# A convolution and an ELU feed-forward layer on one core: another route for the first super tile, and a new order of loads and output turns at the start

## The chip, the cores and the metric

The kernel runs on one core of one Trainium2 chip. Time is device microseconds of one execution; the number that counts is the median over runs. Engines: PE (TensorE; its weight loads are PEld), DVE (VectorE), ACT (ScalarE), POOL (GpSimd) and SP (SyncE, which here only issues DMAs).

## The reference, cut to what matters

```
x: 8 x 4096 x 192 (fp32), weight: 8 heads x 7 taps
w = softmax(weight, over the 7 taps)
a[b, s, h*24 + c] = sum over k of w[h, k] * x[b, s + k - 6, h*24 + c]   # zeros ahead of each batch row
h = a @ w_in            # 32768 x 192  @  192 x 2048
g = h if h > 0 else exp(min(h, 0)) - 1
out = g @ w_out         # 32768 x 2048 @ 2048 x 192, fp32
```

A causal convolution of seven taps along the sequence, one set of taps for each of eight heads of 24 channels; then a feed-forward layer with an ELU.

## The kernel before, in words

The 32768 tokens are 32 super tiles (`s`) of 1024 tokens, each in two groups of 512 (`GS`). The hidden 2048 columns are 16 blocks of 128 (`q`); a step `n = 16 s + q` makes one block of hidden values for both groups, and there are 512 steps. The array is used as two row halves (`tile_position` 0 and 64): the two groups of tokens lie on partitions 0 to 63 and 64 to 127, with the 192 channels cut into three pieces `j` of 64. For that w_in is held twice, in the lower and in the upper 64 rows.

**Convolution** (L622, "c" items). x is loaded by POOL with a cast to bf16 into `xg`, as overlapping windows of 118 tokens, 112 of them new. A banded matrix `Tm` (118 x 112 for each head) turns a window into 112 convolved tokens. A super tile has four convolution units `m`, two heads each, with matmuls on the rows below and above 64. Each unit is evacuated to `csb` (L522 on ACT), and one DMA transpose (L412, issued by SP) then brings the super tile into `att`, channel-major, as the H matmuls need it. The units of super tile s are run some 20 steps ahead of their use, at `CONV_AT`; those of s=1 at the steps `EARLY_CONV`; those of s=0 ahead of everything.

**The band.** The taps are softmaxed on DVE and ACT (`wq` to `wprb`). SP writes zeros to a DRAM tensor `conv_band`, then writes `wprb` along its diagonal, then reads it back into `Tk` (tap-major layout, 128 rows of 1792 bytes). Super tile 0 is convolved with `Tk`; DVE copies it into `Tm` (L561) for the rest.

**H** (L643). Three matmuls of 512 columns (j = 0, 1, 2) for each group; ACT takes exp of the PSUM bank into `E` (L526); POOL clamps E to at most 1 (L499); DVE forms `max(E - 1, H)` into `gT` as fp16 (L575). That is the ELU. A unit of this chain is one (n, group).

**Output** (L666, "o" items). For each half super tile `k` and group `g`, 64 matmuls accumulate over the 16 q in one PSUM bank, in turns of `QB` = 2 blocks a step, starting at step `O_AT` = 12 for group 0 and 16 for group 1. The bank is evacuated by ACT (L530) and stored by SP (L369).

**Order.** A planner in Python at the head of the kernel writes out PE's order: every item gets a due time from a model clock for each row half, items of a step are interleaved by it, and PSUM's eight banks are given out in the order in which the model believes them free. Each engine then works through its own list in order; semaphores hold the dependencies, and PE waits (`wait_bank`) for whatever last used a bank. `warm` puts matmuls on zeros (L605) into the order: 40 at the start, 24 ahead of the first H, two in each of the steps 1 to 11.

**Order of loads.** POOL issues x of super tile 0, the first 8 blocks of w_in (lower rows), waits for them and copies them to the upper rows by DMA, waits for DVE's second csb evacuation, issues x of super tile 1, waits for the transposed `att`, and issues the other half of w_in. x of super tile 2 and w_out are issued among the first steps (`x_before`, `W_OUT_AT`). SP copies the other half of w_in to the upper rows (L716).

Of the kernel before, what the change touches and what calls it, by code (L numbers as in the profile page):

```python
# [27 lines left out]
CU = 4  # L28
# [9 lines left out]
QA = 8  # L38
WARM = (40, 24, 2)
# [6 lines left out]
EARLY_CONV = (3, 4, 6, 7)  # L46
X_AT = ((2, 1, 1), (1, 1, 0))
ZERO_AT = 8
W_OUT_AT = 5
X_EARLY = 7  # L50
X_WHOLE = False
X_OFF = 0


def bass_lightweight_conv__then__act_elu_kernel(
# [100 lines left out]
    def warm(count):  # L156
        what = ("w", len(plan))
        take_bank(what)
        freed[bank_of[what]] = max(clock)
        plan.append((max(clock) - AHEAD, what + (count,)))  # L160
        clock[:] = [max(clock)] * 2
# [11 lines left out]
    def block_items(n, g, rt):  # L173
        k, b = divmod(n - O_AT[g], NB)
        if k < 0:
            return []
        items = o_items(k, g, rt, range(QB * b, QB * (b + 1)), 2 * b + rt, True, True)
        return evacuated(items, k, g) if b == NB - 1 and rt == 1 else items
# [7 lines left out]
    warm(WARM[0])  # L186
    for rt in range(2):
        lists = [[], []]
        for m in range(CU):
            lists[rt] += c_items(m, rt)  # L190
        emit(lists)
        clock[:] = [max(clock)] * 2
    for n in range(NP):
        if n == 0:
            warm(WARM[1])
        elif n < O_AT[0]:
            warm(WARM[2])
        lists = [[], []]
        convs = conv_steps.get(n, [])
        for m in convs:  # L200
            lists[0] += c_items(m, 0)
        lists[0] += block_items(n, 0, 0) + block_items(n, 1, 0) + h_items(n, 0)
        lists[1] += h_items(n, 1)
        for m in convs:
            lists[1] += c_items(m, 1)
        lists[1] += block_items(n, 0, 1) + block_items(n, 1, 1)
        emit(lists)
# [21 lines left out]
    emit(tail)  # L229
    pe_order += [item for _, item in sorted(plan, key=lambda p: p[0])]  # L230
# [24 lines left out]
    x_before = {4: [(2, 0)]}  # L255
    for s in range(2, NS):
        for u, ahead, gr in X_AT:
            before = 0
            for item in act_order:
                before += item[0] == "h"  # L260
                if item == ("c", CU * s + u):
                    break
            if s + ahead < NS:
                x_before.setdefault(before + X_OFF, []).append((s + ahead, gr))
    x_before.setdefault(X_EARLY, []).append((2, 1))
# [4 lines left out]
    band = nc.dram_tensor("conv_band", (P, TW, HEADS), BF16).ap()  # L270

    with ExitStack() as stack:
# [11 lines left out]
        Tk = sbuf("Tk", [P, CW, HEADS], BF16)  # L284
# [8 lines left out]
        wq = sbuf("wq", [P, HEADS, KSIZE], FP32)  # L293
        wmx = sbuf("wmx", [P, HEADS], FP32)
        wq2 = sbuf("wq2", [P, HEADS, KSIZE], FP32)
        wex = sbuf("wex", [P, HEADS, KSIZE], FP32)
        wsum = sbuf("wsum", [P, HEADS], FP32)
        wrs = sbuf("wrs", [P, HEADS], FP32)
        wprb = sbuf("wprb", [P, KSIZE, HEADS], BF16)
# [5 lines left out]
        s_w = [sema(f"s_w{i}") for i in range(3)]  # L305
# [4 lines left out]
        s_tm = sema("s_tm")  # L310
        s_cd = sema("s_cd")
        s_wdp = sema("s_wdp")
# [30 lines left out]
        WCOLS = ((0, P * QA), (P * QA, FF))  # L343
        def x_whole(s):
            return X_WHOLE and 2 < s < NS - 1

        x_need, z_need, z_count = {}, {}, 0
        x_count = [[0, 0] for _ in range(NXB)]
        for s in range(NS):
            z_count += s % SPB == 0  # L350
            z_need[s] = z_count
            for g in range(2):
                if g == 0 or not x_whole(s):
                    x_count[s % NXB][g] += 16 + 16 * ((s, g) in ((0, 0), (NS - 1, 1)))
                x_need[s, g] = x_count[s % NXB][g]

        by_vector = (1, 3)

        def conv_read(W, m):

            if m in by_vector:
                W(s_cd, by_vector.index(m) + 1)
            else:
                W(s_ce, m + 1 - sum(v < m for v in by_vector))
# [9 lines left out]
        def conv_evac(W, m):  # L374

            s, u = divmod(m, CU)
            if s >= 2:
                W(s_att[s % 2], 16 * (s // 2))
# [39 lines left out]
        def _gpsimd(g: bass.BassGpSimd):  # L418
            W = Waits(g)

            def load_x(s, gr):
                b = s % NXB
                if s >= NXB:
                    W(s_cv, CU * (s - NXB) + CU)
                if s == 0 and gr == 0:
                    g.memset(xg[0:PAD, 0, 0, :], 0.0).then_inc(s_z)
                    g.dma_start(
                        xg[PAD:KW, 0, 0, :], x_flat[0 : KW - PAD, :]
                    ).then_inc(s_x[0][0], 16)

                if x_whole(s):
                    if gr == 0:
                        src = bass.AP(
                            tensor=x_flat.tensor,
                            offset=(s * SUP - PAD) * D,
                            ap=[[D, P], [CW * D, NWIN], [GS * D, 2], [1, D]],
                        )
                        g.dma_start(
                            xg[:, b, :, :].rearrange("p (w g) d -> p w g d", g=2), src
                        ).then_inc(s_x[b][0], 16)  # L440
                    return

# [13 lines left out]
                else:  # L456
                    windows(int(s == 0 and gr == 0), NWIN, P)
# [6 lines left out]
            def load_w_in(k):  # L464
                c0, c1 = WCOLS[k]
                for j in range(3):
                    g.dma_start(  # L467
                        w_in[0:HP, j, c0:c1],
# [7 lines left out]
            for gr in range(2):  # L476
                load_x(0, gr)
            load_w_in(0)
            W(s_w[0], 48)
            c0, c1 = WCOLS[0]  # L480
            g.dma_start(w_in[HP:P, :, c0:c1], w_in[0:HP, :, c0:c1]).then_inc(s_wdp, 16)  # L481
            W(s_cd, 2)
            for gr in range(2):
                load_x(1, gr)
            W(s_att[0], 16)
            load_w_in(1)
            for i, (n, u) in enumerate(units):
                s, at_n = divmod(i // 2, NQ)
                if i % 2 == 0:
                    if i // 2 == W_OUT_AT:  # L490
                        g.dma_start(
                            w_out[:, :, :], moe_w_out.rearrange("(q p) d -> p q d", p=FC)
                        ).then_inc(s_w[2], 16)
                    if at_n == ZERO_AT and (s + 2) % SPB == 0 and s + 2 < NS:
                        batch_zeros(s + 2)
# [13 lines left out]
        def _scalar(a):  # L509
            W = Waits(a)  # L510
            a.memzero(scr[:, 0:1]).then_inc(s_scr)
# [3 lines left out]
            a.activation(wex[:], wq2[:], ACT.Exp).then_inc(s_wex)  # L515
            for item in act_order:
                if item[0] == "c":
                    m = item[1]
                    if m in by_vector:
                        continue  # L520
                    W(s_cv, m + 1)
# [13 lines left out]
        def _vector(v):  # L535
            W = Waits(v)
            v.memset(zw[:], 0.0).then_inc(s_zw)  # L537
            W(s_wq, 16)
# [5 lines left out]
                wmx[:, :].unsqueeze(2).to_broadcast([P, HEADS, KSIZE]),  # L544
# [6 lines left out]
            W(s_set, 4)  # L551
            v.tensor_tensor(  # L552
                wprb[:, ::-1, :].rearrange("p k h -> p h k"),
                wex[:],
                wrs[:, :].unsqueeze(2).to_broadcast([P, HEADS, KSIZE]),
                ALU.mult,
            ).then_inc(s_set)
            for m in by_vector:
                W(s_cv, m + 1)
                v.tensor_copy(*conv_evac(W, m)).then_inc(s_cd)  # L560
            v.tensor_copy(  # L561
                Tm[0:KW, :, :].rearrange("p h t -> p t h"), Tk[0:KW, :, :]
            ).then_inc(s_tm)
# [21 lines left out]
        def _tensor(pe):  # L585
            W = Waits(pe)

            def wait_bank(what):
# [3 lines left out]
                if was[0] == "h":  # L592
                    W(s_tt, tt_count(*was[1:]))
                elif was[0] == "c":
# [5 lines left out]
            for item in pe_order:  # L600
                if item[0] == "w":
                    W(s_zw, 1)
                    wait_bank(item[:2])
                    for _ in range(item[2]):
                        pe.matmul(H[:, bank_of[item[:2]], :], zw[:, 0:P], zw[:, 0:GS], start=True, stop=True)  # L605
                elif item[0] == "c":
                    _, m, rt, q = item
                    s, u = divmod(m, CU)
                    if m == 0:
                        W(s_band, 48)  # L610
                    if m == CU:
                        W(s_tm, 1)
# [5 lines left out]
                    else:  # L618
                        W(s_cswap, m + 1)
# [4 lines left out]
                        Tm[rows, h, :] if s else Tk[rows, :, h],  # L624
# [9 lines left out]
                elif item[0] == "h":  # L634
                    _, n, r, j = item
                    s, q = divmod(n, NQ)
                    if j == 0:
                        W(s_w[q // QA], 48)
                        if r == 1:
                            W(s_wdp if q < QA else s_wd, 16)  # L640
                        W(s_att[s % 2], 16 * (s // 2 + 1))
                        wait_bank(item[:3])
                    ins = pe.matmul(  # L643
# [9 lines left out]
                else:  # L653
# [9 lines left out]
                    W(s_w[2], 16)  # L663
# [17 lines left out]
        def _sync(sy):  # L681
            W = Waits(sy)
            sy.dma_start(
                wq[:, :, :].rearrange("p h k -> p (h k)"),
                bass.AP(tensor=weight.tensor, offset=0, ap=[[0, P], [1, HEADS * KSIZE]]),
            ).then_inc(s_wq, 16)
            W(s_zw, 1)
            sy.dma_start(
                band[:, :, :].rearrange("p t h -> p (t h)"), zw[:, :]
            ).then_inc(s_band, 16)  # L690
            W(s_band, 16)
            W(s_set, 5)
# [3 lines left out]
                ap=[[HEADS * (TW + 1), P], [1, KSIZE * HEADS]],  # L696
            )
            sy.dma_start(
                diagonal, wprb[:, :, :].rearrange("p k h -> p (k h)")
            ).then_inc(s_band, 16)  # L700
            W(s_band, 32)
            sy.dma_start(
                Tk[:, :, :], band[:, PAD : PAD + CW, :]
# [3 lines left out]
            for m in range(CU - 1, CU * NS, CU):  # L707
                sync_work.append((unit_at_conv[m], ("c", m)))
            sync_work += [(at, item) for at, item in evacs]
            for _, item in sorted(sync_work):  # L710
                if item[0] == "c":
                    transpose(sy, W, item[1] // CU)
                    if item[1] == CU - 1:
                        W(s_w[1], 48)
                        c0, c1 = WCOLS[1]
                        sy.dma_start(w_in[HP:P, :, c0:c1], w_in[0:HP, :, c0:c1]).then_inc(s_wd, 16)  # L716
# [33 lines left out]
```

## Time and profile before

| | us |
|---|---|
| median of 11 runs (lowest, highest) | 741.45 (740.81, 744.53) |
| the profiled execution | 744.53 |
| its span, first to last instruction | 742.7 |
| PE busy, weight loads beside it | 731.7, 686.8 |
| DVE, ACT, POOL busy | 639.3, 675.0, 670.2 |
| mean granted clock of PE | 0.995 |

The profiled execution is the slowest of the eleven. The page gives the busy time of each engine, the span in 40 slices, the DMA queues, the chain of waits that ended last, the costliest groups of instructions and the DMA issues. A group's row has the line, engine and operation, output and inputs with their shapes, the count, the busy time and mean duration, and the idle time just before them with what ended it. A busy PE is not PE at its peak.

### The profile page before, as it was taken

What the parts mean: (1) busy time and instruction counts of PE and PEld (TensorE: products, weight loads), DVE (VectorE), ACT (ScalarE), POOL (GpSimd) and SP (SyncE); (2) the same over time, 40 slices, a digit from 0 to 9 for tenths busy, and PEclk for the clock granted to TensorE, in tenths of its full rate; (3) what the DMA queues carried; (4) which work ended last, traced back from release to release, by engine and by line L of the source; (5) the groups of instructions that cost most, each with busy time, mean ns of one, the idle gap of its engine ahead of it and who ended that gap; (6) DMA issues with size and microseconds to landing.
All of it is one profiled execution on the core that took longest, in us unless ns stands there. A gap on an engine that the chain in (4) does not pass through costs nothing.

```text
span 742.7 us, 27602 instructions
## 1 busy us (share of the span) xinstructions
PE 731.7 (99%) x11862; PEld 686.8 (92%) x11862; DVE 639.3 (86%) x1034; ACT 675.0 (91%) x1281; POOL 670.2 (90%) x1110
## 2 busy tenths in 40 slices
PE   7989999999999999999999999999999999999998
PEld 3359999999999999999999999999999999999997
DVE  1588988989988989988898998898989889898993
ACT  1479999999999999999999999999999999999993
POOL 2879999999999999999999999999999999999893
PEclk9999999999999999999999999999999999999999
DMA  5865653535553454654353455346355435455212
GB/s 98 122 64 85 94 68 64 95 71 93 85 93 55 78 84 81 85 95 73 58 94 73 92 84 86 65 75 90 75 88 91 70 66 90 76 90 82 68 34 66
DMA packets 135499, 59.32 MB, mean 80 GB/s; under 512 B 101680, under 2 KB 134576, under 8 KB 135376
## 3 DMA queue, kind: packets, MB, share of 16 engines
q1 hardware_dynamic: 90112, 39.68, 24.2%
q0 software_dynamic: 44992, 17.67, 22.9%
q8 instruction: 93, 1.52, 0.8%
q14 instruction: 30, 0.25, 0.1%
q10 hardware_dynamic: 272, 0.20, 0.1%
HBM read 34.80 MB, written 25.45 MB: 81 GB/s over the span
## 4 chain that ended last, share of the span: by engine, by line
PE 94%; DMA 2%; POOL 2%; DVE 1%; ACT 1%; issue 0%; DVEq 0%; SPq 0%
PE H L666 53%; PE H L643 37%; PE H L622 4%; POOL E L499 1%; PE H L605 1%; DMA conv_band<-wprb 1%; DVE gT L575 1%; ACT E L526 1%; DMA Tk<-conv_band 0%; DMA wq<-in_weight_dram 0%; POOL xg L449 0%; ACT csb L522 0%; DVE osb L566 0%; DVE wprb L552 0%; ACT osb L530 0%
## 5 line engine op out<-in xcount | busy, mean ns | idle before, releaser
L575 DVE SCALAR_TENSOR_TENSOR gT<-E,H 128x512 f16<-128x512 f32 x1024 | 633.6, 683 | 76.1 <-POOL E L499 74.6
L666 PE MATMUL H<-w_out,gT 64*128 64x192 f16 x8192 | 680.8, 243 | 2.4 <-DVE gT L575 2.1
L643 PE MATMUL H<-att,w_in 64*128 64x512 bf16 x3072 | 681.4, 377 | 0.6 <-ACT csb L522 0.5
L666 PEld LDWEIGHTS H<-w_out,gT 64*128 64x128 f16 x8192 | 628.7, 94 | 21.0 <-DVE gT L575 2.6
L499 POOL TENSOR_SCALAR E<-E 128x512 f32<-128x512 f32 x1024 | 606.7, 612 | 44.7 <-ACT E L526 32.2
L526 ACT ACTIVATE E<-H 128x512 f32<-128x512 f32 x1024 | 594.2, 601 | 40.7 <-PE H L643 14.6
L643 PEld LDWEIGHTS H<-att,w_in 64*128 64x128 bf16 x3072 | 274.4, 93 | 9.2 <-issue 5.1
L622 PE MATMUL H<-xg,Tm 64*112 64x240 bf16 x496 | 92.4, 266 | 0.6 <-ACT csb L522 0.6
L522 ACT ACTIVATE csb<-H 112x480 bf16<-112x480 f32 x126 | 70.9, 563 | 13.4 <-PE H L622 13.4
L530 ACT ACTIVATE osb<-H 128x384 f32<-128x384 f32 x127 | 61.7, 486 | 7.4 <-PE H L666 7.4
L449 POOL DMA_DIRECT2D xg<-in_x_dram x65 | 59.3, 912 | 6.8 <-DVE csb L560 6.6
L622 PEld LDWEIGHTS H<-xg,Tm 64*112 64x112 bf16 x496 | 57.5, 125 | 3.6 <-ACT csb L522 0.9
L605 PE MATMUL H<-zw 128*128 128x512 bf16 x86 | 24.5, 432 | 1.5 <-DVE zw L537 1.5
L605 PEld LDWEIGHTS H<-zw 128*128 128x128 bf16 x86 | 8.2, 108 | 15.4 <-issue 7.8
L560 DVE CAST csb<-H 112x480 bf16<-112x480 f32 x2 | 1.3, 658 | 12.7 <-PE H L622 12.7
L566 DVE COPY osb<-H 128x384 f32<-128x384 f32 x1 | 0.6, 558 | 8.4 <-PE H L666 8.4
L481 POOL DMA_DIRECT2D w_in<-w_in x1 | 0.7, 680 | 7.0 <-DMA w_in<-in_moe_w_in_dram 7.0
L622 PEld LDWEIGHTS H<-xg,Tk 64*112 64x112 bf16 (+1 forms) x16 | 2.6, 297 | 3.2 <-DMA Tk<-conv_band 3.2
L622 PE MATMUL H<-xg,Tk 64*112 64x240 bf16 (+1 forms) x16 | 2.9, 406 | 2.8 <-DMA Tk<-conv_band 2.8
L467 POOL DMA_DIRECT2D w_in<-in_moe_w_in_dram x6 | 3.5, 599 | 0.9 <-DMA att<-csb 0.9
L561 DVE COPY Tm<-Tk 118x896 bf16<-118x896 bf16 x1 | 2.2, 2184 | 0.0
L539 DVE TENSOR_REDUCE wmx<-wq 128x8 f32<-128x56 f32 x1 | 0.2, 211 | 2.2 <-DMA wq<-in_weight_dram 2.2
(17 smaller groups left out, 7.9 us busy)
## 6 DMA issues: line engine op xcount, KB each, us to landing
out_dram<-osb SPq DMA_DIRECT2D x127, 192.0 KB, 3.5
xg<-in_x_dram POOLq DMA_DIRECT2D x62, 240.0 KB, 5.0
w_in<-in_moe_w_in_dram POOLq DMA_DIRECT2D x6, 128.0 KB, 5.3
w_out<-in_moe_w_out_dram POOLq DMA_DIRECT2D x1, 768.0 KB, 10.3
att<-csb SPq DMA_TRANSPOSE x32, 4.7
xg<-in_x_dram POOLq DMA_DIRECT2D x2, 192.0 KB, 4.3
w_in<-w_in POOLq DMA_DIRECT2D x1, 384.0 KB, 5.2
w_in<-w_in SPq DMA_DIRECT2D x1, 384.0 KB, 4.9
```

Of the source, the lines that this page charges most:

```text
L449: g.dma_start(xg[0:rows, b, 2 * w0 + gr : 2 * w1 : 2, :], src).then_inc(s_x[b][gr], 16)
L467: g.dma_start(w_in[0:HP, j, c0:c1], bass.AP(tensor=moe_w_in.tensor, offset=8 * j * FF + c0, ap=[[CPH * FF, HEADS], [FF, 8], [1, c1 - c0]], ...
L499: g.tensor_scalar(out=E[:, i % NE, :], in0=E[:, i % NE, :], scalar1=1.0, scalar2=0.0, op0=ALU.min, op1=ALU.max,).then_inc(s_clp)
L522: a.activation(*conv_evac(W, m), ACT.Copy).then_inc(s_ce)
L526: a.activation(E[:, i % NE, :], H[:, bank_of[item], :], ACT.Exp).then_inc(s_exp)
L530: a.activation(*out_evac(W, *item[1:]), ACT.Copy).then_inc(s_oev[item[2]])
L561: v.tensor_copy(Tm[0:KW, :, :].rearrange("p h t -> p t h"), Tk[0:KW, :, :]).then_inc(s_tm)
L575: v.scalar_tensor_tensor(out=gT[:, s % NG3, q, u, :], in0=E[:, i % NE, :], scalar=1.0, in1=H[:, bank_of[item], :], op0=ALU.subtract, op1=A ...
L605: pe.matmul(H[:, bank_of[item[:2]], :], zw[:, 0:P], zw[:, 0:GS], start=True, stop=True)
L622: ins = pe.matmul(H[0:CW, bank_of["c", m], 256 * q : 256 * q + UC], Tm[rows, h, :] if s else Tk[rows, :, h], xg[rows, s % NXB, :, CPH * h ...
L643: ins = pe.matmul(H[:, bank_of[item[:3]], :], w_in[HP * r : HP * (r + 1), j, FC * q : FC * (q + 1)], att[HP * r : HP * (r + 1), s % 2, j, ...
L666: ins = pe.matmul(acc_of(k, g)[:, D * kb : D * (kb + 1)], gT[HP * rt : HP * (rt + 1), t % NG3, q, g, t0 : t0 + P], w_out[HP * rt : HP * (r ...
```

## The change

Super tile 0 no longer goes through `xg`, `Tk`, `csb` and the DMA transpose. SP and ACT load its x as fp32 into `xs`; ACT casts it into `xb`, piece by piece in channel order; PE transposes each window by a matmul with an identity (`"t"` items, three pieces of five windows) into PSUM; DVE and ACT copy that to `xT`; then seven matmuls for each piece, each with a diagonal 128 x 128 matrix of one tap (`taps`, made by DVE from the identity) and with xT shifted by one token, add up the convolution channel-major (`"d"` items; the third piece in two halves in two banks); DVE and ACT copy the sums into `att`.

`conv_band` becomes head-major, and `Tm` is read from it directly, 118 rows of eight pieces of 112 elements; `Tk`, L561 and the two csb evacuations on DVE go. The zeros of the band wait for xs to land. The taps are also loaded once per channel (two more DMAs on SP). POOL issues all of w_in, w_out, x(1) and x(2) one after another ahead of its first clamp: w_in's first four blocks go to both row halves straight from DRAM, the other twelve to the lower rows, copied to the upper ones by SP. The first output accumulators start at steps 4 and 8 (`EARLY_O`), one block a step, instead of at 12 and 16 with two; from the second on nothing changes. The early convolutions move from steps 3, 4, 6, 7 to 5, 6, 8, 9. Warm-up is 15 matmuls at the start and two in each of the steps 1 to 3. The planner's model clock is held to at least 1160 ns a step up to step 24.

The diff, cut to its core:

```diff
-QA = 8
-WARM = (40, 24, 2)
+WARM = (15, 2)
+WCOLS = ((0, 4 * FC), (4 * FC, 16 * FC))
-EARLY_CONV = (3, 4, 6, 7)
+EARLY_CONV = (5, 6, 8, 9)
+EARLY_O = (4, 8)
+PACE0, UNTIL = 1160.0, 24
...
         k, b = divmod(n - O_AT[g], NB)
-        if k < 0:
-            return []
+        if k < 1:
+            q = n - EARLY_O[g]
+            if not 0 <= q < NQ:
+                return []
+            items = o_items(0, g, rt, range(q, q + 1), 2 * q + rt, True, True)
+            return evacuated(items, 0, g) if q == NQ - 1 and rt == 1 else items
...
+    start_up = [("t", j) for j in range(3)] + [("d", j) for j in range(3)]
...
     for n in range(NP):
-        if n == 0:
+        if 0 < n < EARLY_O[0]:
             warm(WARM[1])
-        elif n < O_AT[0]:
-            warm(WARM[2])
+        if n < UNTIL:
+            clock[:] = [max(c, PACE0 * n) for c in clock]
...
+    pe_order += [("w", 0, WARM[0])] + start_up
...
-    band = nc.dram_tensor("conv_band", (P, TW, HEADS), BF16).ap()
+    band = nc.dram_tensor("conv_band", (P, HEADS, TW), BF16).ap()
...
# POOL
-            for gr in range(2):
-                load_x(0, gr)
-            load_w_in(0)
-            W(s_w[0], 48)
-            g.dma_start(w_in[HP:P, :, c0:c1], w_in[0:HP, :, c0:c1]).then_inc(s_wdp, 16)
-            W(s_cd, 2)
+            g.memset(ones[:], 1.0).then_inc(s_id)
+            ...
+            g.affine_select(out=ident[:], in_=ones[:], ...)
+            load_w_in(0, 0)
+            load_w_in(0, 1)
+            load_w_in(1, 0)
+            load_w_out(0)
             for gr in range(2):
                 load_x(1, gr)
-            W(s_att[0], 16)
-            load_w_in(1)
+            load_w_out(1)
+            for gr in range(2):
+                load_x(2, gr)
...
# ACT
+            first_window(a, 1, 0, NWIN)
...
+            W(s_xz, 1)
+            W(s_xs, 48)
+            for j in range(3):
+                a.activation(xb[0:CW, j, :, :]..., xs[0:CW, :, :]..., ACT.Copy).then_inc(s_cast)
+            for sem, count, ins in (
+                (s_xt, 3, transposed(2)),
+                (s_first, 1, first_att(0, 0, GS)),
+                (s_first, 3, first_att(2, 0, GS // 2)),
+            ):
+                W(sem, count)
+                a.activation(*ins, ACT.Copy).then_inc(s_fa)
...
# DVE, behind the softmax
+            v.tensor_scalar(out=wch[:], in0=wex[:, HEADS, :], ...)
+            W(s_id, 2)
+            for tap in range(KSIZE):
+                v.tensor_scalar(out=taps[:, tap, :], in0=ident[:], scalar1=wch[:, tap : tap + 1], ...)
+            for j in range(2):
+                W(s_xt, j + 1)
+                v.tensor_copy(*transposed(j)).then_inc(s_fd)
             v.tensor_tensor(
-                wprb[:, ::-1, :].rearrange("p k h -> p h k"),
+                wprb[:, :, ::-1],
...
-            v.tensor_copy(Tm[0:KW, :, :].rearrange("p h t -> p t h"), Tk[0:KW, :, :]).then_inc(s_tm)
+            W(s_first, 2)
+            v.tensor_copy(*first_att(1, 0, GS)).then_inc(s_fd)
+            W(s_first, 3)
+            v.tensor_copy(*first_att(2, GS // 2, GS)).then_inc(s_fd)
...
# PE
+                elif item[0] == "t":
+                    for w in range(NWIN):
+                        ins = pe.matmul(windows_of(j)[:, w, :], xb[0:CW, j, 2 * w : 2 * w + 2, :]..., ident[0:CW, 0:CW], ...)
+                elif item[0] == "d":
+                    first_evacuated(W, ("t", j))
+                    for tap in range(KSIZE):
+                        W(s_tap, tap + 1)
+                        for part in range(2 if j == 2 else 1):
+                            ins = pe.matmul(H[:, bank_of[item] + part, c0:c1], taps[:, tap, :], xT[:, j, tap + c0 : tap + c1], ...)
...
-                    if m == 0:
+                    if m == CU:
                         W(s_band, 48)
-                    if m == CU:
-                        W(s_tm, 1)
...
# SP
+            first_window(sy, 0, 0, 1)
+            first_window(sy, 0, 1, NWIN)
+            for g in range(2):
+                sy.dma_start(wq[HP * g : HP * (g + 1), HEADS, :], ...).then_inc(s_wq, 16)
...
             W(s_zw, 1)
+            W(s_xs, 48)
             sy.dma_start(band..., zw[:, :]).then_inc(s_band, 16)
             W(s_band, 16)
-            W(s_set, 5)
+            W(s_set, 6)
             diagonal = bass.AP(
...
-                ap=[[HEADS * (TW + 1), P], [1, KSIZE * HEADS]],
+                ap=[[HEADS * TW + 1, P], [TW, HEADS], [1, KSIZE]],
             )
+            sy.dma_start(diagonal, wprb[:, :, :]).then_inc(s_band, 16)
+            W(s_w[1], 48)
+            sy.dma_start(w_in[HP:P, :, c0:c1], w_in[0:HP, :, c0:c1]).then_inc(s_wd, 16)
             W(s_band, 32)
-            sy.dma_start(Tk[:, :, :], band[:, PAD : PAD + CW, :]).then_inc(s_band, 16)
+            sy.dma_start(Tm[0:KW, :, :], band[0:KW, :, PAD : PAD + CW]).then_inc(s_band, 16)
```

## The prediction

> **What bounds the kernel now.** I read the page first, then the chain of waits from 0 to 30 us, the timeline of PE and VectorE up to 64 us, and the table of stretches. In the page's costliest groups, one group of 512 columns costs VectorE and PE this:
>
> ```profile
> L575 DVE SCALAR_TENSOR_TENSOR gT<-E,H 128x512 f16<-128x512 f32 x1024 | 633.6, 683 | 76.1 <-POOL E L499 74.6
> L666 PE MATMUL H<-w_out,gT 64*128 64x192 f16 x8192 | 680.8, 243 | 2.4 <-DVE gT L575 2.1
> L643 PE MATMUL H<-att,w_in 64*128 64x512 bf16 x3072 | 681.4, 377 | 0.6 <-ACT csb L522 0.5
> ```
>
> PE stands idle for 3 us in all (last column) behind its two large groups: from 50 us on it is the bound. The table of stretches (busy of PE, PEld, DVE, ACT, POOL; then granted clock, DMA share, GB/s) shows where it is not:
>
> ```profile
> 10.50:11.00 0.50, 0.50 (x4) 0.26 (x3) 0.00 (x0) 0.00 (x0) 0.00 (x0) 1.00 0.13 23
> 16.50:20.50 4.00, 4.00 (x19) 2.63 (x19) 2.45 (x3) 1.04 (x2) 0.83 (x1) 0.59 0.00 0
> 42.50:44.70 2.20, 0.08 (x4) 0.08 (x4) 2.19 (x5) 1.09 (x2) 1.82 (x4) 0.96 0.70 72
> 44.70:48.00 3.30, 3.23 (x23) 2.37 (x25) 1.00 (x2) 1.19 (x2) 1.17 (x2) 0.51 0.22 48
> 64.00:85.88 21.88, 21.88 (x373) 21.33 (x370) 19.75 (x32) 21.06 (x41) 20.66 (x35) 1.00 0.51 80
> ```
>
> One super tile, 16 steps n, takes 21.88 us with PE busy throughout: 1.3675 us a step. Nothing of the change touches this stage. Before it stands the start, a single chain (start, length, what):
>
> ```profile
> 0.75 2.89 DMA wq<-in_weight_dram
> ...
> 5.42 6.87 DMA conv_band<-wprb
> 12.30 3.40 DMA Tk<-conv_band
> 15.71 0.04 issue
> 15.75 2.92 PE H L622 x16
> 18.67 6.28 PE H L605 x24
> 24.95 0.76 PE H L643 x6
> ```
>
> The L605 matmuls are only warm-up: under them lie the csb evacuations, the transposing DMA (issued 19.47, landed 23.4) and its wait. The first H group starts at 24.88. Counting six L643 matmuls a step, n=24 starts at 61.7; 488 further steps at 1.3675 end at 729, where the last L643 matmul indeed is (728.74). So the end is fixed by when n=24 starts: the steps, accumulators and tail from there on are the same in both kernels. I sum only up to n=24.
>
> Steps 0 to 24 take 36.8 us now. In the quiet steps H groups start 1.29 apart (24.88, 26.17, 27.46), VectorE's pace of two gT. That makes 24 x 1.29 = 31.0. The four steps with convolutions of s=1 take 1.52, 2.49, 1.53 and 2.24 (28.76 to 30.28, 32.77; 34.06 to 35.59, 37.83): 2.6 over 4 x 1.29. The rest, 3.2, is the idle PE at 42.5 to 44.7, ahead of the first output turns, and the clock of 0.51 after it.
>
> **Part by part: the first H group.** The change takes the band's round trip through DRAM, 16 matmuls on Tk, four csb evacuations and the DMA transpose out of this chain. It puts in their place:
> - x in fp32, issued from SP and ACT at 0.75 to 1.5. The same source bytes landed 4.5 us (192 KB) and 6.8 us (240 KB) after issue, so between 5.6 and 8; I take 7.0, nearer the second, since w_in shares the engines. The taps' loads stand behind it on SP; alone wq took 2.9, behind x I take 7.0 too.
> - VectorE: wmx to wrs as now, 3.66 to 4.89 = 1.23; wch and seven taps at 0.20 (small rows are 0.20 to 0.22; wprb, with a rearranged output, 0.40) = 1.6, at most 3.2. To 9.9. The first evacuation of 560 columns, by the 0.66 of a 480-column CAST, 0.7: 10.6.
> - Beside that, ACT's three casts of 640 columns (0.7 each by the 0.57 of 480) from 7.3, and 15 small transposing matmuls (0.18 each by the 16 in 2.92): the first is done near 9, hidden behind the taps. Were the taps free, the casts would decide, and only 0.9 earlier.
> - Diagonal matmuls: 14 of 512 and 14 of 256 columns, 21 times 512. Full clock 0.215 (five in 1.24), 4.5 us; half clock 0.427, 9.0. Now 2.75 us of idle PE at 13 bring the clock to 0.50 from 17.2 to 20.6. The new chain has 15 warm-ups instead of 40, done near 7.7, then little until 10.6: I take one such half-rate stretch, 4.5 + 1.7 = 6.2, to 16.8.
> - Last evacuation in halves 0.4, last H matmuls: the group ends at 17.7 against 25.7 now. **8.0 us earlier**, as if it started at 16.9. Bounds from landing and clock: 14 to 20.
>
> **Queues.** POOL issues nine w_in pieces (0.6), w_out in two (1.2 together) and four x loads (0.95) at once: 10.4 us from 1.6 on, finished at 12, and its first clamp comes only near 19. That hides the issues; in return three issues of 0.92 to 1.20 leave the steps themselves. Bytes: x 0.86, w_in 0.98, w_out half 0.39 and x(1) 0.48 MB come to 2.7 MB; at 126 to 184 GB/s that is 15 to 21 us, and with 2 us around it x(1) is there for n=5 at 23.4. At the 112 GB/s of the first 8 us it would be 3 us late. The copy of w_in to the upper rows is issued near 14.5 (4.9 to landing), for n=4 at 22.
>
> **A wait that comes in.** Tm is now read straight from the band: 118 rows of eight 224-byte pieces, 944 in all, where Tk took 128 pieces of 1792 bytes and VectorE's 2.18 us copy. SP orders it last: the zero band waits for x (7.0; then 2.9 to 5), the diagonal for wprb (11.6), issued at 12.1. That diagonal is 1024 pieces of 14 bytes instead of 128 of 112. Below, the 6.87 of now; above, 56 more pieces on each engine at the software queue's mean packet of 60 ns (22.9% of 16 spans over 44992 packets), 10.3; I take 8.0: 20.1. For Tm itself, below Tk's 3.4, above the longest transpose with its 1712 packets, 7.2; I take 5.3: **25.4**. The convolutions of n=5 wait for it on PE in order, and every H group, output turn, and so ACT, POOL and VectorE wait behind them. n=5 is due at 16.9 + 5 x 1.29 = 23.4: a **stall of 2.0**, between 0 and 5.4.
>
> Here a page of the Trainium skill speaks against the change: "DMA: Bandwidth & Descriptors", section "Why a DMA increments its semaphore by 16 and not by 1", says that a transfer is spread over the largest number of engines up to 16 that divides its rows. For 118 rows that would be two engines with 472 pieces each. No run here shows an SP transfer of such a row count. By the rule the total would be that of the first rival or worse.
>
> **Steps 0 to 24 after.** 31.0; for the convolution steps 1.5 (four ACT evacuations of 0.57 less the 0.2 that ACT idles a step; between 0 and 2.6, as POOL's issues are gone); for the accumulators' banks at n=4 and n=8 1.0 (between 0 and today's 3.2: the turns are thinner, one q a step from n=4, and PE has spare time there, since 0.65 of H and 0.33 of output fit in 1.29); stall 2.0. So n=24 starts at 16.9 + 31.0 + 1.5 + 1.0 + 2.0 = 52.4 instead of 61.7: **9.3 us less**. The output turns moved ahead are worth at most the 3.2 in this; they are no time of their own, for n=24 on is PE-bound with the same backlog. The profiled execution took 744.53 (span 742.7, 1.8 around it): 735.2. It lies 3.1 above the median of 741.45, so **732.1**.
>
> **Rivals.** (1) *Tm lands late, still faster.* If few engines carry it: at 10.5 to 11.0 a share of 0.13, two engines of 16, moved 23 GB/s. 211 KB at that are 9.2 us, and 2.0, the shortest landing in the trace: 31.3, a stall of 7.9, and 0.8 for a cooled clock. 9.3 - 5.9 - 0.8 = 2.6 less: 738.9. For it: the load changes from whole rows to small pieces and from 128 rows to 118. Against: 1712 transpose packets land in 3.8 to 7.2.
> (2) *Slower.* The same place, at the software queue's 60 ns a piece: 472 pieces on each of two engines take 28.6, landing at 50.7, a stall of 27: 758. It decides as soon as Tm lands after 33.9, or 13.8 us after its issue; then n=5 gives back all that the start gained. For it: nothing else stands ready on PE behind that wait. Against: a transfer of plain reads without cast should be cheaper a piece than x with its cast.
> (3) *The clock stays at half* through all diagonal matmuls: 9.0 instead of 6.2, less 6.5 in all: 735.0. PEclk after 13 speaks for it; the small transposes between speak against.
> The claim that the chain is not shortened at all has nothing for it: its longest links are gone.
>
> **Numbers.** Forecast 0.46, (3) 0.12, (1) 0.19, slower by (2) 0.18, and 0.05 for a stall that just cancels the gain. 0.2%, or 1.5 us, is about what a measurement of this kernel can tell from no change. Faster 0.77, same 0.05, slower 0.18. Below, no stall, full clock and free banks give 726 to 727; above, the range runs over (1) to the near part of (2): 727 to 744, with some 0.05 below and 0.15 above.
>
> **What would show it.** Right: first L643 near 17, no DMA transpose before it; diagonal matmuls from 10.6 at 0.215 to 0.43 apart; a PE wait at the first L622 of one to three us released by Tm; n=24 near 52; 21.88 a super tile unchanged. Wrong: a Tm wait of 8 us or more at n=5, H groups 1.4 or more apart in quiet steps, a low clock between n=4 and n=12 where the warm-ups are gone, or another period in the steady stage.

## The result and the profile after

| | before | after |
|---|---|---|
| median, us | 741.83 (50 runs) | 745.74 (13 runs) |
| ratio to before, 95% interval | | 1.0046 (1.0032 to 1.0060) |
| profiled execution, its span | 744.53, 742.7 | 746.57, 744.5 |
| first H group starts | 24.88 | 24.28 |
| first convolution of super tile 1 | 28.76 (n=3) | 37.06 (n=5) |
| last H matmul starts | 728.74 | 730.51 |

The kernel became 0.46% slower where 1.3% faster was forecast. The page's groups and the steady stretch of the changed kernel (the columns of the table of stretches as before):

```profile
L650 DVE SCALAR_TENSOR_TENSOR gT<-E,H 128x512 f16<-128x512 f32 x1024 | 633.6, 683 | 74.5 <-POOL E L541 73.0
L778 PE MATMUL H<-w_out,gT 64*128 64x192 f16 x8192 | 684.7, 243 | 0.1
L755 PE MATMUL H<-att,w_in 64*128 64x512 bf16 x3072 | 683.0, 378 | 0.4
L728 PE MATMUL H<-xg,Tm 64*112 64x240 bf16 x496 | 93.4, 268 | 7.5 <-DMA Tm<-conv_band 6.8
```

```profile
26.00:31.00 5.00, 4.25 (x33) 1.47 (x29) 4.28 (x7) 4.36 (x9) 4.63 (x8) 1.00 0.19 29
31.00:37.00 6.00, 0.00 (x0) 0.00 (x0) 2.06 (x4) 0.32 (x1) 1.28 (x3) 0.60 0.15 33
37.20:44.00 6.80, 6.71 (x56) 4.99 (x55) 2.75 (x4) 4.34 (x9) 3.03 (x6) 0.62 0.00 0
64.00:85.88 21.88, 21.88 (x370) 21.01 (x365) 19.77 (x34) 21.07 (x41) 20.64 (x35) 1.00 0.54 80
```

The output turns' wait on gT is gone (2.4 to 0.1 us of idle PE in front of them), and the steady stage is the same 21.88 us. But PE now does nothing from 31 to 37 us, and computes at 0.62 of its clock for the 7 us after. The chain of waits says for what (start, length, what):

```profile
3.08 10.74 DMA wq<-in_weight_dram
15.41 1.23 DVE taps L619 x7
16.64 1.29 DVE xT L628 x2
18.14 6.94 DMA conv_band<-wprb
25.11 11.91 DMA Tm<-conv_band
37.06 0.44 PE H L728
```

Two links are new in size: the taps (`wq`) land 10.7 us after the last issue instead of 2.9, and Tm takes 11.9 where Tk took 3.4. While Tm is loaded, the DMA share is 0.15: little more than two of sixteen engines, for six microseconds. The timeline of PE shows the start:

```profile
15.38 1.81 PE L691 MATMUL H<-ident,xb 112*128 112x112 bf16 x15 [8.80 <-ACT xb L562]
17.35 6.99 PE L706 MATMUL H<-xT,taps 128*128 128x512 bf16 x28 [0.16 <-DVE xT L628]
24.28 1.07 PE L755 MATMUL H<-att,w_in 64*128 64x512 bf16 x6
```

The new route is nearly as short as forecast once it has its inputs: 10.4 us from the taps (13.84) to the first H group, where 9.9 were forecast. It starts 7 us late.

The profiled executions of two of the experiments, e5_pool_waits and b1_turns, were slow ones (1936 and 757 us, their 512-column H matmuls 831 and 386 ns in the mean against 378), so no time is read from these two traces.

### The profile page after: what moved, and what is told of

The parts are those of the page before. It is cut to its first block, busy times and chain, and to the rows that moved or that the text cites. A ratio compares the mean times of both kernels' runs of the same rounds, so it can differ in the third digit from the quotient of the medians.

```text
span 744.5 us, 27549 instructions
## 1 busy us (share of the span) xinstructions
PE 722.9 (97%) x11824; PEld 680.8 (91%) x11824; DVE 639.8 (86%) x1044; ACT 676.6 (91%) x1285; POOL 668.4 (90%) x1111
## 4 chain that ended last, share of the span: by engine, by line
PE 91%; DMA 4%; POOL 2%; ACT 1%; DVE 1%; SPq 0%; issue 0%; DVEq 0%
PE H L778 51%; PE H L755 36%; PE H L728 3%; DMA Tm<-conv_band 2%; DMA wq<-in_weight_dram 1%; POOL E L541 1%; DMA conv_band<-wprb 1%; ACT E L582 1%; DVE gT L650 1%; POOL xg L481 0%; ACT csb L578 0%; SPq L798 0%; DVE xT L628 0%; DVE taps L619 0%; ACT osb L586 0%
## 5 line engine op out<-in xcount | busy, mean ns | idle before, releaser
L728 PE MATMUL H<-xg,Tm 64*112 64x240 bf16 x496 | 93.4, 268 | 7.5 <-DMA Tm<-conv_band 6.8
L728 PEld LDWEIGHTS H<-xg,Tm 64*112 64x112 bf16 x496 | 58.4, 127 | 11.8 <-DMA Tm<-conv_band 7.2
L481 POOL DMA_DIRECT2D xg<-in_x_dram x63 | 56.1, 895 | 0.2 <-issue 0.2
L558 ACT ACTIVATE wex<-wq 128x63 f32<-128x63 f32 x1 | 0.3, 255 | 11.4 <-DVE wq L598 11.4
L691 PE MATMUL H<-ident,xb 112*128 112x112 bf16 x15 | 1.8, 294 | 8.8 <-ACT xb L562 8.8
L685 PE MATMUL H<-zw 128*128 128x512 bf16 x21 | 6.9, 473 | 1.5 <-DVE zw L593 1.5
L706 PE MATMUL H<-xT,taps 128*128 128x512 bf16 (+1 forms) x28 | 7.0, 422 | 0.2 <-DVE xT L628 0.2
L685 PEld LDWEIGHTS H<-zw 128*128 128x128 bf16 x21 | 2.1, 115 | 5.4 <-issue 3.3
L706 PEld LDWEIGHTS H<-xT,taps 128*128 128x128 bf16 x28 | 3.2, 117 | 3.9 <-issue 3.0
## 6 DMA issues: line engine op xcount, KB each, us to landing
w_out<-in_moe_w_out_dram POOLq DMA_DIRECT2D x2, 384.0 KB, 16.7
```

Of the source, the lines that this page charges most:

```text
L481: g.dma_start(xg[0:rows, b, 2 * w0 + gr : 2 * w1 : 2, :], src).then_inc(s_x[b][gr], 16)
L685: pe.matmul(H[:, bank, :], zw[:, 0:P], zw[:, 0:GS], start=True, stop=True)
L691: ins = pe.matmul(windows_of(j)[:, w, :], xb[0:CW, j, 2 * w : 2 * w + 2, :].rearrange("p g c -> p (g c)"), ident[0:CW, 0:CW], start=w in ( ...
L706: ins = pe.matmul(H[:, bank_of[item] + part, c0:c1], taps[:, tap, :], xT[:, j, tap + c0 : tap + c1], start=(tap == 0), stop=(tap == KSIZE ...
L728: ins = pe.matmul(H[0:CW, bank_of["c", m], 256 * q : 256 * q + UC], Tm[rows, h, :], xg[rows, s % NXB, :, CPH * h : CPH * (h + 1)].rearrang ...
```

## The experiments

Each is an edit of the changed kernel, except b1_turns. Each group of runs has its own runs of the kernel before beside it, so kernels are compared through their ratios: "less" is the difference of two ratios times 742. A ratio is uncertain by 0.0014 to 0.0027 either way (1 to 2 us), so a difference of two of them below some 2 us is not told from none. Times are us, in the columns up to "last H" from the profiled execution. "Passed" is the start of the first matmul on Tm (L728; L729 or L730 in some runs).

| run | taps land | first H | passed | last H | median | ratio (95%) |
|---|---|---|---|---|---|---|
| after | 13.8 | 24.3 | 37.1 (n=5) | 730.5 | 745.74 | 1.0046 (1.0032, 1.0060) |
| e1_rows128 | 13.4 | 22.5 | 31.7 (n=5) | 724.2 | 740.14 | 0.9970 (0.9955, 0.9985) |
| e2_wq_first | 8.2 | 20.8 | 34.1 (n=5) | 727.3 | 745.59 | 1.0036 (1.0016, 1.0056) |
| e3_both | 8.7 | 24.2 | 31.4 (n=5) | 723.4 | 739.12 | 0.9951 (0.9934, 0.9969) |
| e4_conv_late | 13.2 | 23.4 | 36.1 (n=9) | 726.1 | 743.17 | 1.0005 (0.9989, 1.0021) |
| e5_pool_waits | | | | | 748.71 | 1.0073 (1.0047, 1.0100) |
| e6_split106 | 11.4 | 20.8 | 34.6 (n=5) | 727.2 | 744.06 | 1.0022 (1.0003, 1.0041) |
| e7_waits_rows128 | 8.3 | 18.2 | 32.2 (n=5) | 725.2 | 741.36 | 0.9987 (0.9967, 1.0008) |
| e9_late_loads | 13.0 | 23.0 | 30.3 (n=5) | 722.8 | 738.84 | 0.9941 (0.9919, 0.9962) |
| g1_best | 11.6 | 21.9 | 31.4 (n=8) | 721.3 | 737.22 | 0.9922 (0.9902, 0.9943) |
| g2_best_waits | 6.9 | 16.7 | 30.5 (n=8) | 721.6 | 736.43 | 0.9910 (0.9889, 0.9931) |
| g3_best_late | 12.3 | 21.5 | 32.6 (n=8) | 722.8 | 739.30 | 0.9952 (0.9935, 0.9969) |

**Is it the number of rows?**

```diff
-    Tm[0:KW, :, :], band[0:KW, :, PAD : PAD + CW]
+    Tm[:, :, :], band[:, :, PAD : PAD + CW]
```

> The changed kernel with one edit: Tm is loaded with all 128 rows of the band instead of 118. Theory (118 rows go to two DMA engines, 128 rows to sixteen): the load, 11.9 us in the changed kernel, lands within 5 us of its issue near 25, so before n=5 is due near 31; the 6.8 us idle PE at the first convolution and the low clock after it go, and the time falls by 6 to 9 us, to 737 to 740. Rival (the 944 pieces of 224 bytes are slow whatever carries them): the load still takes 10 us or more, the wait stays above 5 us, the time stays within 1.5 us of the changed kernel's 745.7.

Ten rows more, and the load takes 7.0 us; the chain of e1_rows128 and PE's waits in it:

```profile
24.57 7.04 DMA Tm<-conv_band
```

```profile
PE H L728 <- DMA Tm<-conv_band: 2.2, 1, 2.2
PE H L755 <- DMA w_in<-w_in: 0.6, 1, 0.6
```

The wait falls from 6.8 to 2.2 us and the time by 0.76%, 5.6 us: just under the theory's 6 to 9, and far from the rival's. Where the 11.9 us went can be read from the DMA packets of the changed kernel. From 28 to 29 us, three microseconds after Tm was issued, only packets of POOL's queue (q0) move; from 31 to 32 us there are only Tm's, on SP's queue (q1) (packets, MB, share of sixteen engines):

```profile
q0 software_dynamic: 64, 0.02, 20.0%
q1 hardware_dynamic: 154, 0.03, 15.4%
```

Tm's first piece moves at 29.5, 4.4 us after its issue, and its 944 pieces take until 36.7. At 154 pieces a microsecond on two engines, a piece costs an engine 13 ns: the pieces themselves are cheap. The trace doesn't name a packet's engine, so what Tm's two engines did before 29.5 isn't seen directly. The rest above 5 us is not the row count; e3 and e9 turn to it.

**Are the taps late by their place in the queue?** SP's loads of the taps are moved ahead of its loads of x; then both edits together.

```diff
-            first_window(sy, 0, 0, 1)
-            first_window(sy, 0, 1, NWIN)
             for g in range(2):
                 sy.dma_start(wq[HP * g : HP * (g + 1), HEADS, :], ...).then_inc(s_wq, 16)
             sy.dma_start(wq[:, 0:HEADS, :]..., ...).then_inc(s_wq, 16)
+            first_window(sy, 0, 0, 1)
+            first_window(sy, 0, 1, NWIN)
```

> The changed kernel with one edit: SP issues the three loads of the taps ahead of its two loads of x. Theory (the taps are late only because their packets stand behind x and between POOL's weight packets): they land by 6 us instead of 13.8, the taps' chain ends before x is cast, the casts then start when x lands (8.5 to 9), the diagonal matmuls start near 11 instead of 17.4, the first H group near 18 instead of 24.3; the band's diagonal is written some 6 us earlier too, so Tm with its 11.9 us lands near 31 and PE still waits some 6 us for it: the time falls by 5 to 7 us, to 739 to 741. Rival (the loads of 28-byte pieces with a repeated source are slow by their form): they still land after 10 us, the first H group stays above 21 us and the time falls by less than 3 us.

> Both edits: the taps' loads first, and Tm with 128 rows. Theory: the two costs add, since one delays the first H group and the other step 5: first H near 18, no PE wait of over 2 us at the first convolution, 12 to 15 us less than the changed kernel: 731 to 734, and 8 to 11 us less than the kernel before. Rival (with the start earlier, the other loads, x of super tile 1 or the copy of w_in to the upper rows, are late in their turn): a wait of 3 us or more for one of them at n=4 or n=5, and 735 to 739.

Neither came as expected. The taps land at 8.2 and 8.7, but now x is last: ACT's casts start at 11.4 in e2 and at 15.0 in e3, where the changed kernel had x by 8.55. In both orders the load issued last is the late one. The two starts are the same code up to the load of Tm, so the 3.6 us between their x are spread between executions, and a single landing at the start is known no better than that. In e2 the first H group is 3.5 us earlier, but PE still stops 5.8 us for Tm (landing in 9.3 us, at 34.1). The traced execution passes the convolution 2.9 us earlier than that of after and is 3.2 us shorter; but it is the shortest of its twelve, and the medians of e2 and after do not differ beyond their intervals. In e3 Tm takes 4.6 us, the first H group is no earlier than in after, and the time is 7.0 us less. So the gain follows the passage of the first convolution, not the first H group.

**Is the stop at n=5 what costs?**

```diff
-EARLY_CONV = (5, 6, 8, 9)
+EARLY_CONV = (9, 10, 11, 12)
```

> The changed kernel with one edit: the convolutions of super tile 1 stand at steps 9, 10, 11, 12 instead of 5, 6, 8, 9; Tm is loaded as in the changed kernel. Theory (the slow load of Tm costs only because PE waits for it in order at n=5): by n=9, due near 36.5, Tm has landed at 37, the wait shrinks from 6.8 to below 2 us, and the time falls by 4 to 7 us, to 739 to 742; att of super tile 1 is then needed at n=16 near 46 and may add a wait of up to 2 us. Rival (the steps to 24 are paced by the other engines, and the wait at n=5 is made good later): the time stays within 1.5 us of 745.7.

PE's wait for Tm falls to 1.7 us, but 0.8 us for att of super tile 1 comes in at n=16, and three of the four convolutions, now in neighbouring steps, put 0.47 us of csb evacuation each on the chain. 3.0 us less than after: between the two expectations; the wait costs, but moving its place returns only part.

**Crowding, or two engines again?** POOL waits ahead of its first load; or the 106-row window goes as 96 and 10 rows; or POOL's wait together with the 128 rows.

```diff
+            W(s_xs, 48)
+            W(s_wq, 48)
             load_w_in(0, 0)
```

```diff
-            first_window(sy, 0, 0, 1)
+            first_window(sy, 0, 0, 1, (16, CW))
+            first_window(sy, 0, 0, 1, (PAD, 16))
```

> The changed kernel with one edit: POOL waits for x of the first super tile and for the taps before it issues its first weight load; SP's order and Tm are as in the changed kernel. Theory (POOL's weight loads, which keep the DMA engines full from 2.5 us on, hold up whatever SP and ACT have issued): x lands by 6 instead of 8.5, the taps by 6.5 instead of 13.8, the first H group starts at 15 to 17 instead of 24.3; the copy of w_in to the upper rows is later, with a wait of 0 to 4 us at n=4, and Tm still takes over 9 us with a wait of 5 to 8 us at n=5: the time falls by 4 to 8 us, to 738 to 742. Rival (the taps are late because two DMA engines have the 106-row window ahead of them): they still land after 10 us and the time does not fall by more than 1.5 us.

> The changed kernel with one edit: the first window of x, 106 rows, is loaded in two transfers, of 96 and of 10 rows; POOL's loads go out as in the changed kernel. Rival of the crowding theory (106 rows go to two DMA engines, and the taps' packets stand behind 53 rows on each): the taps land by 9 us instead of 13.8 and the first H group starts near 20; the time falls by 3 to 5 us. Crowding theory: the taps still land after 11 us, and the time stays within 1.5 us of the changed kernel's 745.7.

> Two edits: POOL waits for x and the taps before its weight loads, and Tm is loaded with 128 rows. Theory (the two costs, crowding at the start and the two-engine load of Tm, together make up what the prediction missed): first H group at 15 to 17, Tm within 7 us of its issue, waits at n=4 and n=5 together below 4 us, n=24 near 53: 731 to 735, 7 to 10 us less than the kernel before. Rival (the bytes needed by n=5 set the pace whatever the order): n=5 starts no earlier than the 31 of the run with 128 rows alone, and the time stays at 739 to 741.

Both causes show: the taps land at 13.0 to 13.8 in the four runs with both, at 11.4 to 12.3 in the three with the window split (e6, g1, g3), at 8.3 without POOL's loads, and at 6.95 in g2 without either. Neither pays much: e6 is 1.8 us less than after, at the edge of the intervals. With POOL waiting the first H group starts at 18.2 and then PE stands at n=4; PE's waits in e7_waits_rows128:

```profile
PE H L757 <- DMA w_in<-w_in: 6.1, 1, 6.1
PE H L730 <- DMA Tm<-conv_band: 0.7, 1, 0.7
```

The time of e7 is no less than that of e1 (1.2 us more, the intervals overlap) although its first H group is 4.4 us earlier; e5, which loads Tm with 118 rows as well, is 2.0 us above after (the intervals overlap too). The rival written for e7 (the bytes needed by n=5 set the pace) gave 31 or later and 739 to 741; measured were 32.2 and 741.4. Its numbers came, but not its reason: e9 below has Tm in at 26.1.

**The output turns alone**, in the kernel before; `block_items` and the model clock are as in the change (the clock counted from the end of the old start), and the warm-ups in the steps end at step 3:

```diff
-W_OUT_AT = 5
+EARLY_O = (4, 8)
+PACE0, UNTIL = 1160.0, 24
...
+            g.dma_start(w_out[:, :, :], moe_w_out.rearrange("(q p) d -> p q d", p=FC)).then_inc(s_w[2], 16)
             W(s_cd, 2)
             for gr in range(2):
                 load_x(1, gr)
```

> The kernel before with one part of the change: the first output accumulators start at steps 4 and 8 with one block a step, the model clock is held to 1160 ns a step up to step 24, the warm-ups end at step 3, and w_out is issued behind the first copy of w_in, ahead of x of super tile 1. The first super tile is as before. Theory (moving the turns ahead removes the idle PE at 42.5 to 44.7 and the half clock after it, and nothing else): 2 to 4 us less than the kernel before, 738 to 740. Rival (w_out ahead of x and w_in makes these late by as much): no change within 1.5 us, or slower.

739.68 us, ratio 0.9957 (0.9938 to 0.9976): 3.2 us less (1.8 to 4.6), and the idle PE and half clock in the old start were priced at 3.2; the medians of this group differ by only 1.5. The trace can't give the size, but it has no PE wait of over 0.3 us from 36 to 60 us, where the kernel before has one of 2.1 for gT.

**What is left, and a better kernel.** e9 takes half of w_out and x of super tile 2 out of the early queue (steps 2, 4 and 6). The others combine 128 rows, the split window, convolutions at 8 to 11 and eight blocks of w_in straight to both halves.

```diff
+                if i == 4: load_w_out(1)
+                if i in (8, 12): load_x(2, i // 4 - 2)
```

```diff
-WCOLS = ((0, 4 * FC), (4 * FC, 16 * FC))
+WCOLS = ((0, 8 * FC), (8 * FC, 16 * FC))
-EARLY_CONV = (5, 6, 8, 9)
+EARLY_CONV = (8, 9, 10, 11)
```

> Two edits: Tm with 128 rows (alone it took 7.0 us and the time fell to 740.1), and POOL issues the second half of w_out at step 2 and x of super tile 2 at steps 4 and 6, instead of ahead of its first clamp. Theory (what is left of Tm's load above the 3.4 us of Tk is POOL's queue: a few engines still carry x of super tile 2 when the rest have finished): Tm lands within 5 us of its issue, the wait at n=5 goes from 2.2 us to below 0.5, 1 to 3 us less: 737 to 739. Rival (the small pieces are what is left, or POOL's three issues of 0.9 to 1.1 us inside the steps cost what the wait gives): Tm stays above 6 us, or no change within 1 us of 740.1.

> Four edits: Tm with 128 rows, the 106-row window in two transfers, the convolutions of super tile 1 at steps 8 to 11, and the first eight blocks of w_in straight to both row halves (so the copy to the upper rows is needed at n=8 instead of n=4). Theory (an earlier first H group pays only if nothing is asked of the copied w_in, of Tm or of x of super tile 1 before it can have landed): first H near 21 as with the split alone, no PE wait of over 1 us up to n=12, n=24 near 54.5: 733 to 736. Rival (the first steps are paced by something else): the first convolution is passed no earlier than 35 or n=24 is not before 57: 738 or more.

> The four edits, and POOL waits for x and the taps before its weight loads. Theory (crowding and the two-engine window both hold up the taps; either alone left them at 8.3 and 11.4 us): with both gone they land by 6.5, the first H group starts near 16.5; the copy of w_in is some 3 us late for n=8, n=24 near 53: 731 to 735. Rival (the taps' own form is slow): they land at 8 us or later, as without the split, and the time is that of the four edits alone or up to 3 us more.

> The four edits, and the second half of w_out and x of super tile 2 issued at steps 2, 4 and 6. Theory: with the convolutions at step 8 Tm is in time anyway, so the later loads bring nothing, and POOL's issues in the steps cost 0 to 1.5 us: 733 to 737. Rival (the backlog of POOL's queue still decides the first steps): 1 to 3 us less than the four edits alone.

e9: Tm lands 3.0 us after its issue and PE has no DMA wait left, 2.2 us less than e1: the other 4 of Tm's 7 us go with POOL's early loads. Tm is in at 26.1, and the first convolution still starts only at 30.3. PE now waits for VectorE's gT there; one of POOL's moved issues (0.88 us) lies in the chain before it:

```profile
23.12 0.58 SPq L828 DMA_DIRECT2D Tm<-conv_band  x1
27.25 0.88 POOL w_out L510
30.26 0.28 PE L729 MATMUL H<-xg,Tm 64*112 64x240 bf16 x1 [1.30 <-DVE gT L651]
```

g1: no DMA wait up to n=12 (Tm is in at 28.3), 1 us above its expected range. g2 is the fastest, 6.7 us under the kernel before (0.9910). Its taps land at 6.95 and its first H group starts at 16.71, 5.2 us ahead of g1's, yet the two differ by 0.8 us in the median, within their intervals. The chain of g2 shows why: SP waits for the last piece of w_in until 19.1 (the band's diagonal is in no earlier: its last packet ends then too), issues the copy of w_in, and Tm, with its 128 rows, then takes 10.5 us behind that copy and beside all that POOL had to issue later.

```profile
3.53 3.42 DMA wq<-in_weight_dram
6.99 0.59 issue
7.59 4.53 POOL w_in L499 x8
12.12 7.01 DMA w_in<-in_moe_w_in_dram
19.14 0.71 SPq L828
19.85 0.05 issue
19.91 10.52 DMA Tm<-conv_band
30.42 0.04 issue
30.46 0.44 PE H L730
```

g3 is 2.2 us slower than g1: with the convolutions at step 8 the later loads bring nothing (Tm lands at 24.8, where g1's 28.3 was early enough), and POOL's three issues (0.88, 0.85 and 0.85 us) lie on the chain of the first steps.

## Why the prediction was wrong, point by point

| step | predicted | measured in after |
|---|---|---|
| x lands; taps land | 7.0; 7.0 | 8.55; 13.84 |
| taps to first diagonal matmul | 3.6 | 3.5 |
| diagonal matmuls | 6.2 | 7.0 |
| first H group starts | as if at 16.9 | 24.28 |
| diagonal written: issue, length | 12.1, 8.0 | 18.14, 6.94 |
| Tm: length, landing | 5.3, 25.4 | 11.91, 37.0 |
| passage of n=5 to the last H matmul | 27.0 + 667.0 = 694.0 | 693.5 |

**Two terms failed, both landings.** The taps were given x's 7.0 us, on the ground that the trace of before showed 2.9 for them alone; behind x with its 106-row window, and with POOL's weight loads on the way, they took until 13.84. And Tm was given 5.3, between Tk's 3.4 and the transposes' 7.2, and took 11.91. Tk has 128 rows; with 128 rows Tm takes 7.0 (e1), and 3.0 with half of w_out and x of super tile 2 out of the way (e9). So 4.9 us of the 11.9 are the 118 rows and some 4 the loads that POOL had issued early, which the sum for Tm did not hold at all. Issue of the diagonal 6.0 us late, its length 1.1 less, Tm 6.6 longer: 11.6 us at n=5. The forecast gain of 9.3 less 11.6 is a loss of 2.3; the profiled spans show 1.8, the medians 3.9, the ratio 3.4. PE's wait for Tm was 6.8 us, under the 8 named as a sign of being wrong, only because the step itself was due late: 24.28 + 5 x 1.29 = 30.7 instead of 23.4.

**The rule that spoke against the change was right.** The Trainium skill's page "DMA: Bandwidth & Descriptors", section "Why a DMA increments its semaphore by 16 and not by 1", gave two engines for 118 rows; the trace shows a DMA share of 0.15 at 33 GB/s while Tm is alone on the way, and ten rows more took 4.9 us off it. Rival (1) had the right place and, by luck, nearly the right price (11.2 us of landing from the 23 GB/s row, 11.9 measured): that row of the old start was a mean over six packets of POOL's queue and eleven of SP's, not a load on two engines, and the measured 11.9 is 4.4 us before the first piece and 7.2 of moving. It also stood on the forecast's early start, which would have left a gain. With the taps late too, the change crossed to rival (2)'s side: Tm at 37.0, behind the decision point of 33.9 named there. Rival (2)'s own price of 60 ns a piece was far too high (13 measured). The probability put on the slower side, 0.18, was low: both rivals of the late Tm were measured against a forecast with the taps in time, and the late taps stood in no rival, only in the bounds of 14 to 20 for the first H group (24.28 measured). Both landings come earlier with POOL's loads out of the way (8.3 for the taps in e7; 3.0 us for Tm in e9), so they were not separate risks.

**The queues.** The bytes were added up for x of super tile 1 and for w_in, and both came about in time (the copy of w_in made PE wait 0.6 us in e1 and 1.3 in e2). What was left out is that a small transfer issued into full engines waits too: the taps here. The same page's section "Issuing engines are not separate DMA queues" says that transfers of SP, ACT and POOL run on the same engines and interleave; the taps' landing at 13.8 beside POOL's loads, against 8.3 when POOL waits (e7), is that rule with this kernel's numbers.

**What held.** The chain from the inputs to the first H group (0.5 us longer); the diagonal matmuls (6.99 where one half-rate stretch gave 6.2); the turns ahead (3.2 us, b1); n=5 to the end; the steady stage. One overlap was not as written: ACT's casts were put beside the taps, from 7.3, but in the kernel they stand behind the taps' exp on ACT and start at 14.52. It cost nothing that shows, for VectorE's seven products of the taps end only at 16.64.

**Where the gain of the start went.** In the runs with the first convolution at n=5 the first H group starts between 18.2 and 24.3 us, and the time from the passage of that convolution to the last H matmul is 693.5, 692.5, 693.2, 692.0, 692.6, 693.0 and 692.5. The end follows the passage to within 1.5 us; the start of H leaves no trace in it. The passage in turn waits for the later of two things. In after, e1, e2 and e6, by 0.3 us in e3, and at n=8 in g2, it is Tm; in e7 first the copy of w_in at n=4 (6.1 us), then Tm. In e9, g1 and g3 it is the first H group and the steps behind it: Tm is in at 26.1, 28.3 and 24.8, three to eight microseconds ahead of its use. No run had both early: g2 and e7 start H at 16.7 and 18.2 and pass at 30.5 and 32.2; e9 and g3 have Tm by 26.1 and 24.8 and start H at 23.0 and 21.5. Whether an order exists that has both stays open: no run shortened the three DMAs through the band in a row, and none issued Tm ahead of SP's copy of w_in.

## What to carry to other kernels

Shortening the chain to the first matmul pays only up to the next thing that the in-order engine asks for: list every landing needed in the first steps with its own issue time, and price the earliest gain by the latest of them. A small transfer at the head of a chain is best on its way before the engines are filled (3.4 us in g2 against 10.7 in after). Bulk loads that are needed late can hold up an early one, but moving them costs too: it brought 2.2 us in e9, where Tm was late, and lost 2.2 in g3, where it was in time. Before a load's row count is trimmed, see that it still divides among the engines: with ten useless rows the kernel here is 5.6 us faster than without.

## What the runs showed of the hardware that was not expected

- 118 rows of eight 224-byte pieces: 11.9 us, at a DMA share of 0.15 while nothing else moved; 128 rows: 7.0 us (e1), 4.6 (e3) and 3.0 (e9), by what else was on the way, but 11.2 in e7 and 10.5 in g2.
- Three small loads of 32 KB in all landed 3.4, 5.2, 7.9 and 10.7 us after the last issue (g2, e7, e6, after), by what else was on the way.
- The zeros for the band, 268 KB, took 2.9 us at an empty start and 10.6 us when POOL's loads were in flight (e6).
